# One store before a turn of the DMA queue, cut unevenly over the DMA engines

## The chip, the cores and the metric

The kernel runs on one core of one Trainium2 chip. The metric is device time in microseconds of one execution of the whole kernel; the median of three runs is compared. A core has five compute engines, which the profile calls PE, DVE, ACT, POOL and SP, and 16 DMA engines that move data between HBM and the on-chip memory of 128 partitions. All large transfers here are issued from one queue, SP's.

## The reference

A channel attention over one image `x` of 384 x 384 pixels and 384 channels in bf16, with a convolution kernel of length k = 1:

```python
g = jnp.einsum("bhwc->bc", x) / (H * W)          # mean of every channel over the image
s = jax.nn.sigmoid(g * w1d[0])                   # k = 1, so no neighbours
return x * s[:, None, None, :]                   # every pixel scaled per channel
```

The image has 113.2 MB. Every element has to be read to form the mean before any element of the output can be written.

## The kernel before

The image is seen as 128 partitions of 1152 rows, a row being one pixel's 384 channels (768 bytes). `load(at, a, n)` at line 279 brings `n` rows into the on-chip `arena` (or `annex`) at place `a`; `store(at, a, n)` at line 535 writes `n` rows back. Each is one DMA over all 128 partitions, issued from SP.

**Pass one** reads the whole image. PE sums all rows into a PSUM bank by matmuls with a matrix of ones (line 292). What fits on chip stays there: the last rows loaded stay raw, and further rows are kept in a folded form, in which the bits of four rows are packed into the room of three by DVE shifts, ands and xors (lines 327 and 333) with a check on ACT (line 364). The remaining rows are streamed through and lost.

**The turn.** When the last row is summed, ACT forms the scale `s_bf` (line 513). DVE multiplies the raw rows by it (line 527, with 15 of the rows on POOL), and they are stored piece by piece. The pieces are listed by hand in `landed`; the last of that list is `(W + 8, raw(W + 8), 6, True)` at line 710, six rows. After these stores come the loads of **pass two**, which reads the streamed rows once more, scales them and stores them, while the folded rows are unfolded, scaled and stored between.

The order of pass two is made by a planner that runs when the program is built (from line 786). It keeps a model of the queue with a row costing 0.2267 us and decides when SP issues a load or a store. The model's costs and so the order do not depend on how `store` cuts its transfer.

`Flow.add` (line 34) records each step with the rows it reads and writes. From them it derives semaphore waits: a load into rows waits for every store that still reads them. Each DMA on a queue takes one of 24 semaphore lanes in turn, and a lane is taken again only when its transfer of 24 DMAs before has landed. At the end each lane's last transfer is waited for (lines 138 to 142).

Of the kernel before, what the change touches and what calls it, by code (L numbers as in the profile page):

```python
# [145 lines left out]
def kernel(  # L146
# [11 lines left out]
    nc = tc.nc  # L158
    P = nc.NUM_PARTITIONS
    B, H, W, C = x.shape  # L160
# [35 lines left out]
    W = A + 3 * PIECE  # L196
# [38 lines left out]
    of = out.rearrange("b h w c -> (b h w) c")  # L235
# [4 lines left out]
    def view(t, r0, n):  # L240
        return t[r0 * P : (r0 + n) * P, :].rearrange("(p r) c -> p r c", r=n)

    def mem(a, n):
        return arena[:, a : a + n, :] if a < X else annex[:, a - X : a - X + n, :]

    def rows(lo, n):
        return [("a", r) for r in range(lo, lo + n)]

    fl = Flow(nc, tc)
# [9 lines left out]
    def run_of(i):  # L259

        return next(run for run in reversed(RUNS) if i >= run[0])
# [81 lines left out]
    def fold(k, T=T, Y=Y):  # L343
# [36 lines left out]
            join(w2, w2, flat(T + i * p, p), XOR, wc[2] + rows(T + i * p, p), wc[2])  # L380


    N_DVE, N_SP = (62, 14), 32

    fl.add("ACT", lambda: nc.scalar.dma_start(out=w_bf[:], in_=w1d.to_broadcast((1, 1))), writes=["w_bf"], dma=True)
# [6 lines left out]
        reads=["ones", "w_bf"], writes=["bank0"],  # L392
# [4 lines left out]
        reads=["bank0"], writes=["w_sc"],  # L397
# [50 lines left out]
    for i, bk in enumerate(banks):  # L448
        lo, hi = i * BANK, min((i + 1) * BANK, PS * C)
# [55 lines left out]
    for a, n in [(X, N_X), (U, 8), (V, 8), (W + 4, 8), (W + 12, 8), (W + 20, 7), (W, 4), (T, 4), (T + 4, 4), (Y, 4), (Y + 4, 2), (Y + 6, 2)]:  # L505
# [8 lines left out]
        reads=["bank0", "w_sc"], writes=["s_bf"],  # L514
# [20 lines left out]
    def store(at, a, n):  # L535
        r0, m = run = run_of(at)
        lo, hi = at - r0, at - r0 + n
        assert hi <= m
        return fl.add(
            "SP",  # L540
            lambda: nc.sync.dma_start(out=view(of, *run)[:, lo:hi, :], in_=mem(a, hi - lo)),  # L541
            reads=rows(a, hi - lo), dma=True,
        )

    def unfold(g, lo, p, n, first, whole):

# [239 lines left out]
    while True:  # L786
        MANY, SHORT, FEW, AMPLE, LOW, LAST = next(r[1:] for r in RULES if todo <= r[0])

        if dve_at <= now:
# [4 lines left out]
            if landed and (ahead < PENDING or not can):  # L794
                a, at, n, end = landed.popleft()
# [13 lines left out]
        if alongside and alongside[0][0] <= now:  # L809
            _, a, at, n = alongside.popleft()  # L810
            store(at, a, n)
            storing = True
            moves.append([now + LAT, n * ROW + PER_STORE, stored(a, n)])
        while waiting and waiting[0][0] <= now:
            if not storing and waiting[0][1] < FEW and todo < N_STREAM and sum(e[1] for e in moves) >= AMPLE:
                break
            _, n, then, at, a, known = waiting.popleft()
            known.append(store(at, a, n))
            storing = True
            moves.append([now + LAT, n * ROW + PER_STORE, then])  # L820
# [7 lines left out]
        if bank_at is None and len(line) <= total - BANKS_AT and got and max(got)[0] >= N_BANKED:  # L828
            a = max(got)[1]
# [3 lines left out]
            for i, bk in enumerate(banks):  # L833
                lo, hi = i * BANK, min((i + 1) * BANK, PS * C)
# [6 lines left out]
        if got and todo < N_STREAM:  # L841
            n, a = max(got)
            left = N_STREAM - todo
            left -= run_of(left - 1)[0]
            n = min(n, CAP, left)
            ahead = backlog()
            behind = storing and sum(m for m, _ in got) < MANY and ahead >= SHORT
            if not behind and (todo or not (landed or alongside or waiting)) and (n >= min(BIG, left) and (n == left or left > CAP) or (ahead < LOW and n >= 8) or ahead < LAST):
                storing = False

                lo = N_STREAM - todo - n
# [51 lines left out]
```

## Time and profile before

| what | value |
|---|---|
| median of 3 runs | 715.07 us (714.80 to 715.54) |
| profiled execution | 714.23 us |
| its span, first to last instruction | 712.4 us |
| DVE busy | 476.3 us (67%) |
| PE busy | 214.5 us (30%) |
| ACT busy | 121.6 us (17%) |
| moved by DMA | 301.34 MB, mean 423 GB/s |
| of it read from and written to HBM | 187.96 MB and 113.25 MB |

The span runs from the first to the last instruction; the execution's time also has what lies around it, 1.8 us. The profile's page cuts the span into 40 equal slices and gives for each the busy share of every engine in tenths; its DMA row is the mean over the 16 DMA engines, and its GB/s row is what they moved. A table of stretches gives the same for chosen windows. Pass one fills the first 267 us or so of the span; the first store of raw rows is issued at 269.19 us, and the first load of pass two at 283.99 us.

### The profile page before, as it was taken

The numbers are of one execution on the slowest core, as the hardware profiler recorded it, in microseconds if no ns is written. First come the engines' busy times: TensorE is split into PE (matmuls) and PEld (weight loads), VectorE is DVE, ScalarE is ACT, GpSimd is POOL, SyncE is SP. The second block draws the span as 40 slices with busy tenths as digits, with TensorE's granted clock in tenths as the row PEclk, the third lists the DMA queues.
The fourth block names the chain that finished last, engine by engine and source line by source line (L and its number), as shares of the span: only waits on it lengthen the run. The fifth ranks groups of instructions, "written<-read, shape, count | busy, mean of one in ns | idle before, by whom it ended". The sixth has DMA issues, their size and how long they took to land.

```text
span 712.4 us, 2053 instructions
## 1 busy us (share of the span) xinstructions
PE 214.5 (30%) x1186; PEld 0.3 (0%) x3; DVE 476.3 (67%) x371; ACT 121.6 (17%) x97; POOL 10.2 (1%) x7
## 2 busy tenths in 40 slices
PE   4686968888887880000000000000000000000000
PEld 0000000000000000000000000000000000000000
DVE  3608250347968947959899989979258914897460
ACT  3706140235746730000000200000000000000000
POOL 0000000000000005000000000000000000000000
PEclk9898989999999995555555555555555555555555
DMA  9999999999999998999999999999999999999997
GB/s 370 443 418 440 429 433 433 433 429 432 426 427 428 434 389 346 393 427 423 430 431 434 428 439 439 430 419 435 445 433 428 437 435 433 430 436 433 425 436 311
DMA packets 17727, 301.34 MB, mean 423 GB/s; under 512 B 1971, under 2 KB 2483, under 8 KB 5811
## 3 DMA queue, kind: packets, MB, share of 16 engines
q1 hardware_dynamic: 17712, 301.21, 99.0%
q8 instruction: 4, 0.07, 0.0%
q14 instruction: 9, 0.07, 0.0%
q10 hardware_dynamic: 2, 0.00, 0.0%
HBM read 187.96 MB, written 113.25 MB: 423 GB/s over the span
## 4 chain that ended last, share of the span: by engine, by line
DMA 71%; DVE 16%; PE 7%; ACT 2%; SPq 0%; issue 0%; DVEq 0%
DMA arena<-in_x_dram 47%; DMA out_dram<-arena 19%; DVE arena L527 10%; PE bank L292 7%; DMA annex<-in_x_dram 3%; DVE arena L327 2%; ACT arena L364 2%; DVE annex L527 2%; DVE arena L333 1%; DMA out_dram<-annex 1%; SPq L286 0%; ACT s_bf L513 0%; SPq L541 0%; SPq L898 0%; DVEq L124 0%
## 5 line engine op out<-in xcount | busy, mean ns | idle before, releaser
L527 DVE TENSOR_TENSOR arena<-arena,s_bf 128x6144 bf16<-128x6144 bf16 (+9 forms) x69 | 212.1, 3114 | 84.4 <-DMA arena<-in_x_dram 73.1
L292 PE MATMUL bank<-arena,ones 128*128 128x384 bf16 x1091 | 197.3, 343 | 39.2 <-DMA arena<-in_x_dram 38.4
L327 DVE TENSOR_SCALAR arena<-arena 128x1536 uint16<-128x1536 uint16 (+4 forms) x198 | 136.9, 745 | 105.5 <-DMA arena<-in_x_dram 97.7
L364 ACT ACTIVATE arena<-arena 128x3072 uint16<-128x3072 uint16 (+1 forms) x38 | 107.6, 2831 | 105.6 <-DVE arena L327 105.5
L607 PE MATMUL bank<-odd,ones 128*128 128x1 bf16 x1 | 0.2, 187 | 385.9 <-DVE odd L602 385.9
L333 DVE TENSOR_TENSOR arena<-arena 128x1536 uint16<-128x1536 uint16 (+3 forms) x83 | 106.6, 1284 | 9.2 <-PE bank L292 6.2
L445 ACT COPY arena<-bank 128x512 uint32<-128x512 uint32 (+3 forms) x9 | 4.5, 497 | 127.1 <-DMA out_dram<-arena 126.9
L527 DVE TENSOR_TENSOR annex<-annex,s_bf 128x3840 bf16<-128x3840 bf16 x6 | 12.7, 2153 | 10.5 <-DMA annex<-in_x_dram 10.5
L527 POOL TENSOR_TENSOR arena<-arena,s_bf 128x1536 bf16<-128x1536 bf16 (+1 forms) x3 | 10.0, 3356 | 268.6 <-ACT bank L517 268.6
L292 PE MATMUL bank<-annex,ones 128*128 128x384 bf16 x60 | 11.9, 361 | 4.5 <-DMA annex<-in_x_dram 4.5
L445 ACT COPY bank<-arena 128x512 uint32<-128x512 uint32 (+3 forms) x9 | 4.1, 491 | 35.8 <-PE bank L292 35.8
L527 DVE TENSOR_TENSOR arena<-arena,bank 128x1536 bf16<-128x1536 bf16 (+2 forms) x7 | 8.2, 1232 | 0.0
L364 ACT ACTIVATION_READ_ACCUMULATOR arena<-arena 128x1 f32 x38 | 7.1, 186 | 0.0
L292 PE MATMUL bank<-zeros,ones 128*128 128x384 bf16 x32 | 5.5, 326 | 0.0
L527 DVE TENSOR_TENSOR annex<-annex,bank 128x3840 bf16<-128x3840 bf16 x2 | 4.2, 2145 | 0.0
L306 PE MATMUL bank<-arena,ones 128*128 128x384 bf16 x1 | 0.5, 479 | 7.8 <-DMA arena<-in_x_dram 7.8
L513 ACT ACTIVATE s_bf<-bank,w_sc 128x384 bf16<-128x384 f32 x1 | 0.6, 581 | 9.7 <-PE bank L292 9.7
L871 ACT ACT_TABLE_LOAD x1 | 1.3, 1283 | 0.7 <-PEq L887 0.7
L396 DVE TENSOR_SCALAR w_sc<-bank 128x1 f32<-128x1 f32 x1 | 0.2, 159 | 1.1 <-PE bank L391 1.1
L386 DVE MEMSET ones<- 128x128 bf16 x1 | 0.2, 165 | 1.0 <-SPq L118 1.0
L391 PE MATMUL bank<-w_bf,ones 1*128 1x1 bf16 x1 | 0.2, 182 | 2.1 <-DMA w_bf<-in_w1d_dram 2.1
L607 PEld LDWEIGHTS bank<-odd,ones 128*128 128x128 bf16 x1 | 0.1, 105 | 643.6 <-DVE odd L602 643.6
(11 smaller groups left out, 1.5 us busy)
## 6 DMA issues: line engine op xcount, KB each, us to landing
arena<-in_x_dram SPq DMA_DIRECT2D x17, 4608.0 KB, 30.2
out_dram<-arena SPq DMA_DIRECT2D x7, 4608.0 KB, 30.0
out_dram<-arena SPq DMA_DIRECT2D x6, 3072.0 KB, 33.0
arena<-in_x_dram SPq DMA_DIRECT2D x5, 3072.0 KB, 15.2
arena<-in_x_dram SPq DMA_DIRECT2D x6, 2304.0 KB, 20.9
annex<-in_x_dram SPq DMA_DIRECT2D x6, 1920.0 KB, 11.0
arena<-in_x_dram SPq DMA_DIRECT2D x2, 4512.0 KB, 25.9
out_dram<-arena SPq DMA_DIRECT2D x2, 4512.0 KB, 18.6
```

Source lines behind the costliest of these rows:

```text
L292: return pe.add_instruction(mybir.InstMatmult(name=nc.get_next_instruction_name(), ins=[pe.lower_ap(rhs), pe.lower_ap(ones[:])], outs=[pe. ...
L306: return nc.tensor.matmul(acc, lhsT=ones[:], rhs=mem(i, 1)[:, 0, :], start=first, stop=last)
L327: lambda: nc.vector.tensor_scalar(out=dst, in0=src, scalar1=s0, scalar2=s1, op0=op0, op1=op1),
L333: "DVE", lambda: nc.vector.tensor_tensor(out=dst, in0=a, in1=b, op=op), reads=reads, writes=writes
L364: lambda: nc.scalar.activation(out=y, in_=y, func=ACTF.Copy, accum_out=seen[:, 2 * k + i : 2 * k + i + 1]),
L386: fl.add("DVE", lambda: nc.vector.memset(ones[:], 1.0), writes=["ones"])
L391: lambda: nc.tensor.matmul(votes, lhsT=ones[0:1, :], rhs=w_bf[0:1, 0:1], start=True, stop=True),
L445: "ACT", lambda: nc.scalar.copy(dst.bitcast(u32), src.bitcast(u32)), reads=reads, writes=writes
L513: lambda: nc.scalar.activation(out=s_bf[:], in_=acc, func=ACTF.Sigmoid, scale=w_sc[:, 0:1]),
L527: lambda: vec.tensor_tensor(out=v, in0=v, in1=s[:, None, :].to_broadcast([P, n, C]), op=Op.mult),
L607: lambda: nc.tensor.matmul(votes, lhsT=ones[:], rhs=odd[:], start=True, stop=True),
L871: nc.scalar.preload_act_table(ACTF.Sigmoid)
```

## The change

`store` gets an inner helper that issues one DMA for a range of rows and a range of partitions. For the one store of six rows at `W + 8`, the last three rows go first, cut into partitions 0 to 118, 119 to 126 and 127, as three DMAs; the other three rows follow as one DMA over all partitions. A transfer of 119 partitions runs on 7 of the 16 DMA engines, one of 8 partitions on 8, and one of a single partition on 1. All other stores are as before. The first load of pass two is the next transfer on SP.

```diff
+    N_UNEVEN, SHARES = 3, ((0, 119), (119, 127), (127, 128))
     N_DVE, N_SP = (62, 14), 32
...
-        return fl.add(
-            "SP",
-            lambda: nc.sync.dma_start(out=view(of, *run)[:, lo:hi, :], in_=mem(a, hi - lo)),
-            reads=rows(a, hi - lo), dma=True,
-        )
+
+        def put(lo, hi, p0, p1):
+            return fl.add(
+                "SP",
+                lambda: nc.sync.dma_start(
+                    out=view(of, *run)[p0:p1, lo:hi, :], in_=mem(a + lo - (at - r0), hi - lo)[p0:p1]
+                ),
+                reads=rows(a + lo - (at - r0), hi - lo), dma=True,
+            )
+
+        if a == W + 8 and n == 6:
+            cut = hi - N_UNEVEN
+            for p0, p1 in SHARES:
+                put(cut, hi, p0, p1)
+            hi = cut
+        return put(lo, hi, 0, P)
```

## The prediction

> **What bounds the kernel now.** I read the page's busy shares first, then its slices, then the transfers, then a table of stretches of pass two.
>
> ```profile
> span 712.4 us, 2053 instructions
> ...
> PE 214.5 (30%) x1186; PEld 0.3 (0%) x3; DVE 476.3 (67%) x371; ACT 121.6 (17%) x97; POOL 10.2 (1%) x7
> ...
> DMA  9999999999999998999999999999999999999997
> GB/s 370 443 418 440 429 433 433 433 429 432 426 427 428 434 389 346 393 427 423 430 431 434 428 439 439 430 419 435 445 433 428 437 435 433 430 436 433 425 436 311
> DMA packets 17727, 301.34 MB, mean 423 GB/s; under 512 B 1971, under 2 KB 2483, under 8 KB 5811
> ```
>
> No compute engine is busy for more than 67% of the span, while the DMA row is full. The low slices are the first, slices 15 to 17 (about 249 to 303 us, where pass one ends and pass two begins) and the last. So a change moves the time only by the bytes of the DMA engine that finishes last, or by the rate at which the engines get through a stretch.
>
> The packets give the layout. There are 124 big transfers; each ends with one tiny packet per DMA engine (about 124 x 16, the 1971 under 512 B), and the remaining 15,756 packets are about 124 x 128: one packet per partition, 8 for each of the 16 engines.
>
> Next come the rates by stretch and the tail. The last two columns are the DMA share and GB/s; a packet counts where it starts.
>
> ```profile
> 276.00:287.00 11.00, 0.00 (x0) 0.00 (x0) 8.65 (x8) 0.00 (x0) 2.98 (x1) 0.50 1.02 424
> 287.00:291.00 4.00, 0.00 (x0) 0.00 (x0) 3.93 (x4) 0.00 (x0) 0.00 (x0) 0.50 1.05 374
> 291.00:297.00 6.00, 0.00 (x0) 0.00 (x0) 5.90 (x8) 0.00 (x0) 0.00 (x0) 0.50 1.00 427
> 297.00:302.00 5.00, 0.00 (x0) 0.00 (x0) 4.26 (x3) 0.00 (x0) 0.00 (x0) 0.50 1.00 344
> 302.00:316.00 14.00, 0.00 (x0) 0.00 (x0) 10.88 (x6) 0.00 (x0) 0.00 (x0) 0.50 1.02 431
> 316.00:320.00 4.00, 0.00 (x0) 0.00 (x0) 0.00 (x0) 0.00 (x0) 0.00 (x0) 0.50 1.02 415
> ...
> 328.00:332.00 4.00, 0.00 (x0) 0.00 (x0) 3.97 (x3) 0.00 (x0) 0.00 (x0) 0.50 0.97 404
> ...
> 344.00:350.00 6.00, 0.00 (x0) 0.00 (x0) 5.21 (x4) 0.00 (x0) 0.00 (x0) 0.50 0.98 411
> ...
> 480.00:700.00 220.00, 0.19 (x1) 0.10 (x1) 142.77 (x62) 0.00 (x0) 0.00 (x0) 0.50 1.00 433
> ```
>
> ```profile
> 707.00:707.50 0.50, 0.00 (x0) 0.00 (x0) 0.00 (x0) 0.00 (x0) 0.00 (x0) 0.50 0.00 0
> 707.50:708.00 0.50, 0.00 (x0) 0.00 (x0) 0.00 (x0) 0.00 (x0) 0.00 (x0) 0.50 0.32 132
> 708.00:709.00 1.00, 0.00 (x0) 0.00 (x0) 0.00 (x0) 0.00 (x0) 0.00 (x0) 0.50 0.00 0
> 709.00:709.50 0.50, 0.00 (x0) 0.00 (x0) 0.00 (x0) 0.00 (x0) 0.00 (x0) 0.50 0.31 132
> ```
>
> Two facts follow. First, the rate is 433 GB/s for the 220 us up to 700, but dips while the DMA share stays near 1: the engines are occupied, yet slow. The dips lie near places where the queue turns from stores to loads or back. The last raw store gives way to the first load of pass two in the 374 stretch; that load's successor gives way to the next stores in the 344 stretch. Against 433 they cost (433 - 374) x 4 / 433 = 0.55, (433 - 344) x 5 / 433 = 1.03, 0.17 (at 415), 0.27 (at 404) and 0.30 us (at 411). That is 2.32 us, two thirds of it in the first two, and from 480 there is nothing left to lose although the queue turns there too. Second, the engines don't end together. After 707.0 just two 132 GB/s x 0.5 us = 66 KB portions start, which is two packets of 33 KB each time (the last store has 43 rows of 768 B per partition). So two engines run alone, 2 to 3 us behind the other fourteen, and they set the end.
>
> My reading is that while all sixteen engines change direction in the same microsecond they slow each other, and as they drift apart the turns become free. That is an inference from the fading dips.
>
> **The change part by part.** The last raw store (`W + 8`, six rows) is a 576 KB transfer, 128 packets of 4608 B. It becomes 119, 8 and 1 packets of 2304 B (three rows) and then 128 packets of 2304 B. Nothing else in the order is changed.
>
> *Bytes per engine.* One engine moves 433 / 16 = 27.1 GB/s, so a 2304 B packet is 0.085 us and the old share 16 such units. Taking the 7, 8 and 1 engines as nested sets, six engines get 17 + 1 + 8 = 26 units, one gets 27, one gets 9 and eight get 8. So seven engines are delayed by 10 units, 0.85 us (one 0.94), and the other nine are relieved by 7 or 8, 0.60 to 0.68 us. The two groups then reach the first load about 1.53 us apart. In a sentence by itself: the Trainium skill, "DMA: Bandwidth & Descriptors", section on why a DMA increments its semaphore by 16, says the engine count is the largest one up to 16 that divides the slowest dimension and that these are the lowest-numbered engines, which would make the sets nested; no run so far shows which engines they are.
>
> *Small packets.* The nearest row is the 276 to 287 stretch of small stores, 424 against 433, so 2%. The slow group now spends 26 x 0.085 = 2.2 us there: 0.05 us, doubled for the halved packets, +0.1 us. Its ends are 0 and 0.2.
>
> *Three more issues on SP.*
>
> ```profile
> 279.70 4.18 SPq L541 DMA_DIRECT2D out_dram<-arena  x4
> 281.26 1.35 DVE L527 TENSOR_TENSOR arena<-arena,s_bf 128x2304 bf16<-128x2304 bf16 x1
> 283.99 1.18 SPq L286 DMA_DIRECT2D annex<-in_x_dram  x1
> 284.93 1.50 DVE L327 TENSOR_SCALAR arena<-arena 128x1536 uint16<-128x1536 uint16 x3 [2.32 <-DMA out_dram<-arena]
> ...
> 290.16 0.34 SPq L286 DMA_DIRECT2D arena<-in_x_dram  x1
> ...
> 292.30 0.34 SPq L541 DMA_DIRECT2D out_dram<-arena  x1
> ```
>
> ```profile
> L541 SPq DMA_DIRECT2D out_dram<-arena x45: 332/332/1257, 269.2 to 688.3; - x45
> ```
>
> An issue took 0.33 us at the median and 1.26 at most; the four ahead of the load took 4.18 us together, about 1.05 each, so three more cost 1.0 to 3.8 us on SP, and I take 3.2. The load's issue moves from 283.99 to about 287.2, behind three new transfers. Cover: the first of those four stores landed at 284.90 (it released DVE, idle until 284.93), and the other three, 5 + 8 + 6 rows of 128 x 768 B, are 1.87 MB, 4.3 us at 433 GB/s, so work lasts to 289.2. The relieved engines run out about 0.65 us sooner, at 288.6. Cost taken: 0; with the dearest issues (287.8 plus 1.2) the load comes at 289.0, so at most 0.4 us, less than their relief.
>
> *Waits behind it.* The second load (290.16) reuses rows of this store and now waits for all four parts, whose last lands about 0.85 us later, so it issues at 291.0. The first load's 20 rows (a 1.97 MB transfer) keep the engines until 289.2 + 4.5 = 293.7, and the next item on SP, the store at 292.30, waits for DVE anyway. Nothing. If that cover were gone the cost would be the same 0.85. Later transfers keep their order; their semaphore lanes shift by three, and a lane comes round only after 24 transfers: nothing.
>
> *The turns.* This is the unknown. The trace has no case of two groups 1.5 us apart, so bounds: none of the 2.32 us of dips saved, or all of it. A second instant of turning could also cost another 2.32. I take half, because half the engines turn at a time and because later turns, which I take to be spread, lost 0.17 to 0.30 against 0.55 and 1.03: (0.55 + 1.03 + 0.17 + 0.27 + 0.30) / 2 = -1.16 us.
>
> *The tail.* I keep it: the last engines end 2 to 3 us behind the leaders, as now, whichever they are. The leaders' end then carries the sum. If the two present stragglers are among the nine relieved and nothing else changes, the end moves by -0.68; if among the seven, by +0.85.
>
> **Sum.** -0.68 (leaders' bytes) + 0.10 + 0 + 0 - 1.16 = -1.74 us. The profiled execution took 714.23 us (span 712.4 and 1.8 around it), 0.84 below the median of 715.07; the same difference applied to the median gives 713.3 us. For this kernel 0.2%, or 1.43 us, is about what a measurement can tell from no change.
>
> **The rivals.**
>
> *A, the turns are spread* (forecast): 713.3. For it: the dips shrink from 1.03 to 0.17 while the DMA share stays full. Against: the fading rests on five dips, and no row shows that the drift is its cause.
>
> *B, only bytes move.* The turns cost what they cost because of the traffic, not the simultaneity; the sum is between -0.68 and +0.85 by where the stragglers sit: 714.4 to 715.9, no measurable change. For it: the stretch from 297 to 302 slows well inside a load, not exactly at its edge. The Trainium skill, "DMA: Bandwidth & Descriptors", section on rules for kernel authors, speaks against the change: it wants one transfer over 128 partitions and says of splitting by partitions that it isn't worth the bother. By that rule the whole 10 units of the loaded engines would be loss. As a mechanism of this kernel that is the +0.85 end, 715.9; the trace before has only transfers over 128 partitions and can't judge it.
>
> *C, two instants of turning instead of one.* Each group's turn slows the other, so the dips are paid twice: +2.32 - 0.68 = +1.64, 716.7, slower. It decides against the change once the second instant costs more than (1.43 + 0.68) / 2.32, nine tenths of the first. For it: in the 374 stretch even an engine that is still storing is busy and slow. Against: the two stragglers of today turn apart from the rest, and after 480 the sum of all shows no dip.
>
> *D, the tail closes as well.* If the loaded seven stay at 1.53 us and nobody falls back further, a tail of about 2.5 becomes 1.5, another -1.0: 712.3.
>
> **How the numbers follow.** A 0.42, B 0.32, C 0.13, D 0.13. A passes the bound of 1.43 us if more than (1.43 + 0.10 - 0.68) / 2.32 = 0.37 of the dips is saved; I give that 0.32 of its 0.42. Faster is 0.32 + 0.13 (D) = 0.45, same 0.10 + 0.32 (B) = 0.42, slower 0.13 (C). The range goes from 711.3 (D with all dips gone: -0.68 - 2.32 - 1.0, short by 0.3) to 716.0 (B's upper end); what is left out is most of C and little of D.
>
> **What would show it.** Right: in the stretches 287 to 291 and 297 to 302 the rate is well above 374 and 344 with the dips lower in sum; the load's issue is 1 to 4 us later without the DMA share falling; the tail has about seven engines, not two, running last; the end is 1 to 2 us sooner. Wrong: the same dips or twice as many of them (B, C), a DMA share clearly under 1 around 288 to 290 (the issues were not covered), or a tail longer than 3 us.

## The result: 5 us slower, and the profile after

The changed kernel took 720.3 us (median of 4 runs, 719.4 to 721.7) against 714.93 us before (4 runs), a ratio of 1.0077 with a 95% interval of 1.0064 to 1.0091. Run again later, beside other kernels on one chip, it took 718.61 us (9 runs, 716.8 to 719.8) against 713.87: 1.0054 (1.0036 to 1.0072). (A correction to the kernel's description above: POOL scales 13 of the raw rows, 4 + 4 + 5, not 15.)

The page of the first profile: the span is 5.2 us longer, the bytes are the same, and the DMA row is still full.

```profile
span 717.6 us, 2056 instructions
...
DMA  9999999999999989999999999999999999999997
GB/s 367 442 430 435 438 427 428 436 423 433 423 432 427 431 345 394 355 423 421 407 431 424 428 437 437 415 397 433 438 434 433 433 432 438 427 439 436 422 439 309
DMA packets 17870, 301.34 MB, mean 420 GB/s; under 512 B 1986, under 2 KB 2498, under 8 KB 5954
```

Below is the table of stretches that the prediction used, now of the changed kernel (last columns: DMA share, GB/s).

```profile
276.00:287.00 11.00, 0.00 (x0) 0.00 (x0) 8.65 (x8) 0.00 (x0) 2.95 (x1) 0.50 1.02 426
287.00:291.00 4.00, 0.00 (x0) 0.00 (x0) 3.93 (x4) 0.00 (x0) 0.00 (x0) 0.50 0.90 260
291.00:297.00 6.00, 0.00 (x0) 0.00 (x0) 5.90 (x8) 0.00 (x0) 0.00 (x0) 0.50 1.01 405
297.00:302.00 5.00, 0.00 (x0) 0.00 (x0) 4.23 (x3) 0.00 (x0) 0.00 (x0) 0.50 0.99 353
302.00:316.00 14.00, 0.00 (x0) 0.00 (x0) 10.88 (x6) 0.00 (x0) 0.00 (x0) 0.50 1.00 422
316.00:320.00 4.00, 0.00 (x0) 0.00 (x0) 0.00 (x0) 0.00 (x0) 0.00 (x0) 0.50 1.04 413
...
328.00:332.00 4.00, 0.00 (x0) 0.00 (x0) 3.93 (x6) 0.00 (x0) 0.00 (x0) 0.50 1.02 406
...
344.00:350.00 6.00, 0.00 (x0) 0.00 (x0) 5.90 (x6) 0.00 (x0) 0.00 (x0) 0.50 0.96 354
...
480.00:700.00 220.00, 0.18 (x1) 0.10 (x1) 147.29 (x64) 0.00 (x0) 0.00 (x0) 0.50 1.00 433
```

The stretch behind the cut fell from 374 to 260 GB/s, and here the DMA share fell with it, to 0.90. Of the later dips the one at 344 to 350 us went from 411 to 354 with the share near 1. Up to 700 us the rate is 433 again. Two coarse rows split the loss, first of the kernel before, then of the changed one:

```profile
280.00:306.00 26.00, 0.00 (x0) 0.00 (x0) 22.73 (x20) 0.00 (x0) 0.00 (x0) 0.50 1.01 402
310.00:480.00 170.00, 0.00 (x0) 0.00 (x0) 150.81 (x87) 4.48 (x9) 0.00 (x0) 0.50 1.01 430
```

```profile
280.00:306.00 26.00, 0.00 (x0) 0.00 (x0) 20.59 (x19) 0.00 (x0) 0.00 (x0) 0.50 0.98 378
310.00:480.00 170.00, 0.00 (x0) 0.00 (x0) 148.42 (x86) 4.48 (x9) 0.00 (x0) 0.50 1.01 422
```

At the cut (402 - 378) x 26 / 433 = 1.4 us went, in the turns up to 480 us (430 - 422) x 170 / 433 = 3.1 us. In what follows these two rows are called the cut row and the turns row; 1 GB/s is 0.06 us in the first and 0.39 us in the second. In the second profile of the changed kernel, 715.0 us long, they read 377 and 429: the cost at the cut repeated (1.5 us), that of the turns did not (0.4 us). That execution took 716.8 us and was the quickest of its nine. So the turns row differs by 7 GB/s between two executions of one kernel, which is as much as between most kernels below.

The finer windows of the changed kernel at the cut:

```profile
287.50:288.00 0.50, 0.00 (x0) 0.00 (x0) 0.50 (x1) 0.00 (x0) 0.00 (x0) 0.50 0.41 65
288.00:288.50 0.50, 0.00 (x0) 0.00 (x0) 0.50 (x2) 0.00 (x0) 0.00 (x0) 0.50 0.42 92
288.50:289.00 0.50, 0.00 (x0) 0.00 (x0) 0.50 (x1) 0.00 (x0) 0.00 (x0) 0.50 0.81 175
```

And the timeline of its SP queue there (start, duration, queue, line, operation):

```profile
279.68 7.78 SPq L544 DMA_DIRECT2D out_dram<-arena  x7
287.56 0.37 SPq L286 DMA_DIRECT2D annex<-in_x_dram  x1
292.03 0.34 SPq L286 DMA_DIRECT2D arena<-in_x_dram  x1
```

For one microsecond the DMA share is 0.41 to 0.42, or 7 of 16 engines: the seven with the 119 partitions work, and the nine others have nothing, since the transfer of the other three rows is the last of seven issues that took 7.78 us (four took 4.18 before). The load was issued at 287.56 and its first packet started at 289.95 by the trace's packet records.

### The profile page after: what moved, and what is told of

Read it like the earlier page. It is cut to its first block, busy times and chain, and to the rows that moved or that the text cites. A ratio compares the mean times of both kernels' runs of the same rounds, so it can differ in the third digit from the quotient of the medians.

```text
span 717.6 us, 2056 instructions
## 1 busy us (share of the span) xinstructions
PE 212.0 (30%) x1186; PEld 0.3 (0%) x3; DVE 476.5 (66%) x371; ACT 121.5 (17%) x97; POOL 10.2 (1%) x7
## 4 chain that ended last, share of the span: by engine, by line
DMA 71%; DVE 16%; PE 7%; ACT 2%; SPq 0%; issue 0%; DVEq 0%
DMA arena<-in_x_dram 47%; DMA out_dram<-arena 19%; DVE arena L528 10%; PE bank L292 7%; DMA annex<-in_x_dram 3%; DVE arena L327 2%; ACT arena L364 2%; DVE annex L528 2%; DMA out_dram<-annex 1%; DVE arena L333 1%; SPq L286 0%; ACT s_bf L514 0%; SPq L544 0%; SPq L910 0%; DVEq L124 0%
## 5 line engine op out<-in xcount | busy, mean ns | idle before, releaser
L292 PE MATMUL bank<-arena,ones 128*128 128x384 bf16 x1091 | 194.8, 341 | 40.8 <-DMA arena<-in_x_dram 40.2
L306 PE MATMUL bank<-arena,ones 128*128 128x384 bf16 x1 | 0.5, 480 | 8.3 <-DMA arena<-in_x_dram 8.3
```

Source lines behind the costliest of these rows:

```text
L292: return pe.add_instruction(mybir.InstMatmult(name=nc.get_next_instruction_name(), ins=[pe.lower_ap(rhs), pe.lower_ap(ones[:])], outs=[pe. ...
L306: return nc.tensor.matmul(acc, lhsT=ones[:], rhs=mem(i, 1)[:, 0, :], start=first, stop=last)
```

## The experiments

Two quantities are read from every trace. The first is the spread: the time from the first to the last of the 16 completion marks that the engines leave when the first load of pass two has landed. The second is the pair of rows just defined. All ratios are to the kernel before, run beside it on the same chip. In six profiles the first store of raw rows was issued 0.7 to 2.5 us later than in the kernel before, ahead of anything changed, so the rows are compared and not the spans. A profile is one execution and not always a typical one: that of the cut into 112 and 16 partitions took 715.4 us against a median of 718.85, that of the changed kernel with the load held 720.3 us against 717.58.

| kernel | ratio (95%) | cut row GB/s | spread, us | turns row GB/s |
|---|---|---|---|---|
| before | 1 | 402 | 0.57 | 430 |
| two even parts | 1.0008 (0.9996 to 1.0019) | 402 | 0.69 | 431 |
| four even parts | 1.0040 (1.0010 to 1.0070) | 401 | 0.57 | 431 |
| load late | 1.0021 (0.9994 to 1.0048) | 400 | 0.63 | 431 |
| load held | 1.0014 (0.9998 to 1.0031) | 373 | 0.56 | 431 |
| cut four stores sooner | 1.0037 (1.0022 to 1.0051) | 380 | 0.65 | 430 |
| cut at 545 us | 1.0021 (1.0011 to 1.0030) | 406 | 0.64, cut later | 432 |
| changed | 1.0077 (1.0064 to 1.0091) | 378 | 1.30 | 422 |
| changed, again | 1.0054 (1.0036 to 1.0072) | 377 | 1.25 | 429 |
| 112 and 16 partitions | 1.0077 (1.0060 to 1.0094) | 386 | 1.82 | 429 |
| one uneven row | 1.0065 (1.0045 to 1.0084) | 388 | 2.12 | 424 |
| extra transfer | 1.0061 (1.0044 to 1.0077) | 389 | 2.62 | 426 |
| 119 partitions alone | 1.0060 (1.0043 to 1.0077) | 388 | 3.72 | 425 |
| changed, load held | 1.0044 (1.0028 to 1.0059) | 348 | 0.39 | 432 |
| extra transfer, load held | 1.0067 (1.0051 to 1.0084) | 347 | 0.31 | 432 |
| parts from ACT | 1.0057 (1.0038 to 1.0076) | 330 | 2.87, then empty | 432 |
| cut at 354 us | 1.0030 (1.0020 to 1.0040) | 404 | 0.54, cut later | 428 |

**First group: the issues or the unevenness?** Two even parts of three rows, and four even parts of 1, 1, 1 and 3 rows, in place of the uneven ones:

```diff
-            cut = hi - N_UNEVEN
-            for p0, p1 in SHARES:
-                put(cut, hi, p0, p1)
-            hi = cut
+            put(hi - 3, hi, 0, P)
+            hi -= 3
```

```diff
-            cut = hi - N_UNEVEN
-            for p0, p1 in SHARES:
-                put(cut, hi, p0, p1)
-            hi = cut
+            for i in (1, 2, 3):
+                put(hi - i, hi - i + 1, 0, P)
+            hi -= 3
```

> The six rows go as two transfers of three rows over all 128 partitions: one more issue than before, no uneven share. Both theories: the load's issue moves by about 1.2 us, still ahead of the end of the stores, so 714.5 to 715.8 us, as before. If splitting alone costs, it shows here.

> Four transfers (1, 1, 1 and 3 rows) over all 128 partitions: as many issues as the changed kernel, every engine with equal shares. Theory ISSUE (three more issues of about 1.2 us delay the first load, the engines run dry and the later turns are met at a worse moment): 719 to 721 us, load issued at about 287.5. Theory UNEVEN (the seven-engine transfer and the spread of the engines it leaves make the turns dearer): 714.8 to 716 us.

Two parts: 714.34 us, no difference. Four parts: 715.46 us, with the load issued about as late as in the changed kernel, yet without the microsecond at a share of 0.41. SP's timeline of the kernel with four even parts:

```profile
280.42 7.43 SPq L544 DMA_DIRECT2D out_dram<-arena  x7
287.95 0.39 SPq L286 DMA_DIRECT2D annex<-in_x_dram  x1
```

And its windows:

```profile
287.50:288.00 0.50, 0.00 (x0) 0.00 (x0) 0.50 (x1) 0.00 (x0) 0.00 (x0) 0.50 1.05 442
288.00:288.50 0.50, 0.00 (x0) 0.00 (x0) 0.47 (x2) 0.00 (x0) 0.00 (x0) 0.50 0.80 266
288.50:289.00 0.50, 0.00 (x0) 0.00 (x0) 0.50 (x1) 0.00 (x0) 0.00 (x0) 0.50 1.14 384
```

Its cut row is 401, so in this execution the same number of issues did no harm while each transfer fed all sixteen engines. But three of its ten executions took 720.7 to 721.4 us, as long as the theory ISSUE asked, and the rest 713.6 to 716.2; no profile caught a long one, so for those three the issues are not ruled out.

The parts of 8 and 1 partitions left out, and the three parts issued from ACT's queue (`q` is `nc.scalar` for them):

```diff
-    N_UNEVEN, SHARES = 3, ((0, 119), (119, 127), (127, 128))
+    N_UNEVEN, SHARES = 3, ((0, 119),)
```

```diff
-                lambda: nc.sync.dma_start(
+                lambda: q.dma_start(
```

> The parts of 8 and 1 partitions are left out (nine partitions of three rows are not written), so only one more issue than before, with the full unevenness. ISSUE: 714.8 to 716.5 us, the load issued at about 285.2. UNEVEN: 718 to 721 us.

> The three uneven parts are issued from ACT's queue, so SP has no more issues than before; the bytes of each engine are those of the changed kernel. ISSUE: the load is issued near 284, so 714.5 to 716.5 us. UNEVEN: 718 to 721 us.

718.16 us and 718.1 us, both as the unevenness theory asked, but the second for another reason. On ACT's queue the 17 packets of each engine took turns with the first load's, so they landed as late as 294.5 us and the part of a single partition at 296.4 us. The second load, which needs their rows, was issued at 296.41 instead of 290.16, and the queue ran empty: a cut row of 330 GB/s. After that gap its turns row is 432, the first hint that a common restart heals the turns.

**Second group: seven engines, place, or lateness?** Parts of 112 and 16 partitions, which both can use 16 engines; the uneven cut moved to the third store of 48 rows (about 545 us) or to the ten annex rows four stores sooner; and the kernel before with its first load delayed by 120 satisfied waits on SP.

```diff
-    N_UNEVEN, SHARES = 3, ((0, 119), (119, 127), (127, 128))
+    N_UNEVEN, SHARES = 3, ((0, 112), (112, 128))
```

```diff
-        if a == W + 8 and n == 6:
+        big.append(n == 48)
+        if n == 48 and sum(big) == 3:
```

```diff
-        if a == W + 8 and n == 6:
+        if a == X + 10 and at == raw(X + 10):
```

```diff
+                if not todo:
+                    fl.hold("SP", 120, scales[0])
                 load(lo, a, n)
```

> The three rows are cut into 112 and 16 partitions instead of 119, 8 and 1: both parts can run on 16 engines (7 and 1 packets each), so every engine has equal shares, but an engine's partitions are others than in a transfer over 128. Two more issues than before. SEVEN ENGINES (the loss comes from seven engines carrying 17 packets while nine wait, and from the spread this leaves): 714 to 715.5 us, like the even cut. PARTITIONS (the loss comes from splitting by partitions as such, because engines then reach for partitions that are not their own): 717 us or more.

> The uneven cut is moved to the last three rows of the third store of 48 rows, issued about 545 us, where SP has over 10 us to spare, the queue holds over 20 us of work and no turn after it was slow; the store at the turn is whole again. TRANSFER (the cost is the transfer's own): the seven engines' extra 10 packets, 0.85 us, or 2 us if those packets are slow, 715 to 716.3 us. TURN (the cost is made by the place, ahead of the first load and ahead of the dear turns): 714 to 715 us.

> The uneven cut is moved to the store of ten annex rows issued at about 278, four stores ahead of the load, with 7 rows following it; the store at the turn is whole. Work queued behind it covers the issues, so no engine should wait for the next transfer's issue right after it. DRY (the loss begins because nine engines wait for the next issues): under 716 us. SPREAD (the spread of the engines makes the later turns dearer): 717.5 to 721 us, with the first load's landing spread over 1.5 us or more.

> The kernel before, with SP held by 120 satisfied waits ahead of the first load of pass two, about 3 to 4 us; no store is cut. If being late with the load is enough to make the later turns dear: 717.5 to 721 us. If not, only the time that the queue stands empty: up to 2 us, 714.5 to 716.5 us.

The cut into 112 and 16 partitions was the surprise: 718.85 us, as slow as the changed kernel, although all 16 engines left completion marks on both of its parts. So my theory that seven engines do it fell; cutting by partitions at this place is enough. Its engines land the first load 1.82 us apart. The Trainium skill, "DMA: Bandwidth & Descriptors", section on rules for kernel authors, advises one 128-partition transfer over two to disjoint partition halves; this run, with parts of 112 and 16, agrees, with a loss of 0.77%. Its profile shows (402 - 386) x 26 / 433 = 1.0 us of that at the cut and 0.4 us in the turns, but in an execution 3.5 us quicker than the median, so where the rest goes is not shown.

With the uneven cut at 545 us the kernel took 715.09 us, 1.5 us (0.8 to 2.1) more by its ratio. That lies in the range of TRANSFER, but most of it is not in the transfer. The row from 600 to 640 us, first of the kernel before, then of that with the cut at 545 us:

```profile
600.00:640.00 40.00, 0.00 (x0) 0.00 (x0) 37.96 (x17) 0.00 (x0) 0.00 (x0) 0.50 1.00 433
```

```profile
600.00:640.00 40.00, 0.00 (x0) 0.00 (x0) 36.46 (x16) 0.00 (x0) 0.00 (x0) 0.50 1.00 421
```

The 12 GB/s are (433 - 421) x 40 / 433 = 1.1 us. By the packet records they went in the last packets of a load, just ahead of a change back to stores: 16 packets that started from 614.2 to 615.6 us took up to 2.8 us each, where 1.36 us is usual and the kernel before had none longer. So here, too, a turn behind the cut became dear, some 40 us after the cut had landed, and the later ones did not.

Four stores sooner the cut costs 2.6 us (716.42 us), between what DRY and SPREAD asked, so neither forecast was met. The two rows of that kernel:

```profile
281.00:282.00 1.00, 0.00 (x0) 0.00 (x0) 1.00 (x2) 0.00 (x0) 0.00 (x0) 0.50 0.40 106
282.00:294.00 12.00, 0.00 (x0) 0.00 (x0) 7.33 (x8) 0.00 (x0) 0.00 (x0) 0.50 1.02 407
```

Engines ran dry behind this cut as well, for a microsecond at a share of 0.40, and (402 - 380) x 26 / 433 = 1.3 us went in the cut row. Its spread of 1.3 us closed to 0.65 us by the first load while the share was 1.02, so without the queue coming to rest, and its turns row is 430.

The late load was issued at 287.88 us, 3.9 us late, and cost nothing that the rows show (one of its ten executions took 723.0 us, the others 713.2 to 715.2). In that profile lateness did not make the turns dearer.

**Third group: is it the spread?** The changed kernel with the first load held until all parts have landed; the kernel before with the same hold; the kernel before with one more transfer of 119 partitions ahead of the last raw store, which only adds spread and bytes; and the changed kernel again.

```diff
-            writes=rows(a, hi - lo), dma=True,
-        )
+            writes=rows(a, hi - lo), dma=True, after=gate,
+        )
+        gate.clear()
...
-                put(cut, hi, p0, p1)
-            hi = cut
+                gate.append(put(cut, hi, p0, p1))
+            gate.append(put(lo, cut, 0, P))
+            return gate[-1]
```

```diff
+        if a == W + 8 and n == 6:
+            dummy.append(fl.add(
+                "SP", lambda: nc.sync.dma_start(out=view(of, *RUNS[0])[0:119, 0:3, :], in_=mem(0, 3)[0:119]),
+                reads=rows(0, 3), dma=True,
+            ))
...
-            reads=rows(a, hi - lo), dma=True,
+            reads=rows(a, hi - lo), dma=True, after=dummy if at == 0 else (),
```

> The changed kernel, with the first load of pass two held until all parts of the cut store have landed, so that all engines start it together. SPREAD (engines that meet a turn apart make the later turns dear): about 2 us more idle time than the changed kernel at the turn, but the loss after it falls back to that of the kernel before: 716.5 to 719 us, no dearer than the changed kernel. If the spread doesn't matter and lateness does: 721 to 724 us.

> Control: the kernel before, its first load held until the whole store has landed; nothing is cut. Both: only the engines' empty time from the store's landing to the load's first packet, 1.5 to 2.5 us: 715.5 to 717 us, and later turns as before.

> The kernel before with one more transfer ahead of the last raw store: 119 partitions of three rows, from rows at rest to rows of the output that the last store writes over; seven engines get 17 packets more, nothing waits for it but that last store. One more issue, no store cut. SPREAD: the engines reach the first load 1.5 us apart or more, and the later turns get dearer: 717 to 720 us. If the spread itself costs nothing: the extra bytes, at most 1.5 us: 714.5 to 715.7 us.

> The changed kernel once more, beside the others on one chip: 719 to 722 us. SPREAD: in a second profile the loss of the first turn repeats within 0.3 us, that of the later turns within 1.5 us.

In the two diffs `gate` holds the parts of the last raw store, and the first load waits for them. The hold took 3.2 us at the cut of the changed kernel ((402 - 348) x 26 / 433), more than twice what the cut itself takes, and still the kernel wasn't slower than the changed one: 717.58 us. Its spread is 0.39 us and its turns row 432. The extra transfer alone made 718.83 us from a kernel in which nothing was cut, with 426 in the turns. The changed kernel again took 718.61 us, just under the 719 to 722 asked; its cut row repeated within 1 GB/s, but the turns differed by 2.7 us, more than the 1.5 asked.

**Fourth group: the square, another place, another size.** The extra transfer together with the hold (both of the last two edits, the gate with the extra transfer in it); the uneven cut at the first store of 24 rows (about 354 us); and one uneven row in place of three.

```diff
-        if a == W + 8 and n == 6:
+        mids.append(n == 24)
+        if n == 24 and sum(mids) == 1:
```

```diff
-    N_UNEVEN, SHARES = 3, ((0, 119), (119, 127), (127, 128))
+    N_UNEVEN, SHARES = 1, ((0, 119), (119, 127), (127, 128))
```

> The kernel with one more seven-engine transfer ahead of the last raw store, and the first load held until that transfer and the store have landed. With the kernel before, the held load alone and the extra transfer alone this makes a square. SPREAD: the later turns fall back: 430 to 432 GB/s from 310 to 480 us where the extra transfer alone had 426; 717 to 719 us in all, since the held load itself costs 3 to 4 us. If the extra transfer costs something else than spread, 425 to 428 GB/s and 720 us or more.

> The uneven cut on the last three rows of the first store of 24 rows, issued about 354 us, with work queued and SP free; the store at the turn is whole. SPREAD: the turns from 360 to 480 us get dearer, 425 to 429 GB/s from 310 to 480 us, 716 to 718.5 us. If only the stretch right behind the first turn is sensitive: the bytes alone, as in the kernel with the cut at 545 us, 714.5 to 716 us and 430 GB/s or more.

> The changed kernel with one uneven row instead of three: a third of the extra bytes on seven engines, as many issues. SPREAD: a spread of about 0.5 us over what there is, 429 to 431 GB/s from 310 to 480 us, and 715 to 717 us. If the number of parts decides and not their bytes: as the changed kernel, 718 us or more.

The square of hold and extra transfer is the cleanest reading of the rows. The two rows of the kernel with the load held, of that with the extra transfer, and of that with both:

```profile
280.00:306.00 26.00, 0.00 (x0) 0.00 (x0) 21.04 (x19) 0.00 (x0) 0.00 (x0) 0.50 0.95 373
310.00:480.00 170.00, 0.00 (x0) 0.00 (x0) 150.44 (x87) 4.47 (x9) 0.00 (x0) 0.50 1.01 431
```

```profile
280.00:306.00 26.00, 0.00 (x0) 0.00 (x0) 21.06 (x20) 0.00 (x0) 1.20 (x1) 0.50 1.00 389
310.00:480.00 170.00, 0.00 (x0) 0.00 (x0) 149.86 (x87) 4.47 (x9) 0.00 (x0) 0.50 1.01 426
```

```profile
280.00:306.00 26.00, 0.00 (x0) 0.00 (x0) 20.55 (x19) 0.00 (x0) 0.70 (x1) 0.50 0.90 347
310.00:480.00 170.00, 0.00 (x0) 0.00 (x0) 152.23 (x88) 4.46 (x9) 0.00 (x0) 0.50 1.01 432
```

The extra transfer takes 4 GB/s off the turns (1.6 us), and a common start of the first load gives it back in full, at the price of 2.5 us more at the cut than the extra transfer alone. The ratios alone don't tell the square from a plain sum: they are 1.0014 for the hold, 1.0061 for the extra transfer and 1.0067 for both, where the two add up to 1.0075 and each is good to 0.0017. The reading rests on the rows, with one profile for each kernel.

One uneven row cost as much as three (718.54 us): its turns row is 424, lower than I asked of a third of the bytes. Its spread is 2.12 us, made by three late engines and not by seven, so the number of uneven bytes doesn't set the spread. The cut at 354 us cost 2.1 us (1.0030), less than the 716 us and more that I asked for by the median (715.43), but at the expected place: the turns right behind it. The row from 360 to 400 us of the kernel before, and then of that with the cut at 354 us:

```profile
360.00:400.00 40.00, 0.00 (x0) 0.00 (x0) 39.42 (x25) 4.00 (x8) 0.00 (x0) 0.50 1.01 433
```

```profile
360.00:400.00 40.00, 0.00 (x0) 0.00 (x0) 37.84 (x23) 3.99 (x7) 0.00 (x0) 0.50 1.01 420
```

The 13 GB/s are (433 - 420) x 40 / 433 = 1.2 us. The load ahead of that dip landed with a spread of 2.1 us; in the kernel before the same load landed with 2.5 us, and no dip followed. So the spread from first to last mark does not set the price by itself.

No version beat the kernel before; the nearest, two even parts, equals it.

## Why the prediction was wrong

It forecast 713.3 us with a range to 716.0; the time was 720.3. Two steps failed. The turns were put at -1.16 us and cost 3.1 us in one profile and 0.4 us in the other, and the three more issues were put at 0 and cost 1.4 to 1.5 us at the cut. The relief of -0.68 us brought nothing. The end that it gave for its slow rival C, 716.7, was short too.

*Bytes per engine: right in layout, wrong in effect.* The completion marks of the three parts come from 7, 8 and 1 engines. (Each part leaves one early mark besides, which I take for the remaining counts of 16: the 119-partition part has one at 284.02 and seven from 289.6 to 291.2 us.) But two groups 1.53 us apart did not reach the end of the first load: in the first profile fifteen engines land it within 0.62 us and one 0.68 us later. And the relief of -0.68 for the nine others was never collected, because they had to wait for the next transfer.

*Issues on SP: the time was right, the cover wrong.* I put the load's issue at 287.2 and it came at 287.56. I took the cost as 0 because 4.3 us of stores were still queued. That counted work for the average engine. Half of the last store had become work for seven engines, and the other half sat in the fourth of the issues, so nine engines ran dry before that transfer arrived, not before the load: shares of 0.41 and 0.42 for 1 us. Four even parts with the same issues left the cut row at 401. I had also counted from the end of an issue to the start of its data as nothing; here it was 2.0 us (287.93 to 289.95), and 0.6 us on an empty queue (289.75 to 290.37, the kernel with the load held).

*The waits behind it: near.* The second load was issued at 292.03, not 291.0, since the last of the four parts landed at 292.01, and it was covered as said: the first load landed at 295.3 to 296.6 us.

*The turns: wrong in sign, and in the first profile the largest error.* I took -1.16 us from the fading of the dips, reading it as engines drifting apart and so disturbing each other less. The measured term in the first profile is +3.1 us from 310 to 480 us, and +0.4 in the second. Drift is not what makes turns cheap: with the cut at 545 us the engines land every transfer from the first load to 480 us within 1 us of each other, and the turns row is 432, a little above the 430 of the kernel before, in which the spread grows from 0.7 to 2.5 us over the dips from 316 to 350 us. What makes the dips fade instead I can't name.

Of the kernels with something changed at the first turn, all with a spread up to 0.7 us at the first load have 430 to 432 GB/s in the turns, and all with 1.25 us or more have 422 to 429, but for the one with parts from ACT, whose queue then ran empty (432). The two where a hold closed a spread are at 432. The hold and the extra transfer are the direct tests: in these profiles adding spread there made the following turns dearer, and a common start made them as cheap as before, with the cut and with the extra transfer alike. That much is shown by rows of single executions, of which two of one kernel differ by 7 GB/s. A hold also empties the queue, so a spread that closes and a queue that comes to rest aren't told apart by it; for the spread speaks the cut four stores sooner, whose spread closed without a rest. The size of the spread is not the whole measure, since the kernel before carries 2.5 to 3.0 us of it from 347 us on, in one or two late engines, and runs at 433 from 480 us; whether the number of late engines decides is open.

By what means the engines slow each other is open as well. The slow packets stand ahead of the change of direction: in the kernel before, 26 of the 128 packets of the second load took 1.0 to 1.6 us instead of 0.77. They started from 297.7 to 300.3 us, and the first packet of the next store started at 300.9. They were slow before this queue had any work in the other direction under way that the records show, which a clash of directions, the premise of the forecast and of rival C, does not explain.

*The tail: wrong in who, right in length.* I expected seven late engines. The last windows of the changed kernel:

```profile
713.00:714.00 1.00, 0.00 (x0) 0.00 (x0) 0.00 (x0) 0.00 (x0) 0.00 (x0) 0.50 0.23 99
714.00:714.50 0.50, 0.00 (x0) 0.00 (x0) 0.00 (x0) 0.00 (x0) 0.00 (x0) 0.50 0.00 0
714.50:715.00 0.50, 0.00 (x0) 0.00 (x0) 0.00 (x0) 0.00 (x0) 0.00 (x0) 0.50 0.15 66
```

Three packets of 33 KB start in the first, one in the last. By the marks of the last store thirteen engines ended by 713.56 us, two at 715.0 and one at 716.2: three stragglers and not seven, 1.5 to 2.7 us behind, where the two before were 2.2 us behind. The uneven share was no lasting shift.

*The rivals.* C, with a chance of 0.13, had the right side: turns that get dearer when engines meet them apart. Its mechanism, that each group's change of direction slows the other, is not shown, and its size was short, since it left out the empty engines at the cut. B and D fell.

## What to carry to other kernels

When a queue must stay full, ask for each DMA engine by itself what is queued on it; work that seven engines hold covers nothing for the other nine. Where loads and stores alternate closely, hand transfers over whole: in the profiles here cuts by rows over all 128 partitions cost nothing, while cuts by partitions put the engines out of step, and part of the price came in the turns behind. Take more than one profile before reading a few GB/s, since two executions of one kernel differed by as much as two kernels. Before building on a reading such as "drift makes it cheaper", try the opposite sign on the same rows: nothing in them told the two apart.

## What I had not expected of the hardware

A cut into parts that both use all 16 engines (112 and 16 partitions) was as dear as the uneven one, 1.0077. The spread has no fixed price: behind the cuts at 354 and at 545 us one turn each became dear (420 and 421 GB/s over 40 us) with a spread of 2.1 and 1.6 us ahead of it, while the kernel before takes its turns from 480 us on at 433 GB/s with 3.0 us. And at the turn from loads to stores near 300 us of the kernel before, the slow packets came ahead of the first packet in the other direction. Last, the time from the start of an issue to its first packet was 1.0 us for a load issued alone on an empty queue (289.40 to 290.37, the kernel with the load held) but 2.4 us behind three parts on few engines (287.56 to 289.95).
